# Statistics of two tiles formed at once, one projection moved forward, and new instruction orders in a tuned attention and MLP kernel

## The chip, the cores and the metric

The kernel runs on one core of a Trainium2 chip. The metric is the device time of one execution in microseconds (us). A profile shows one execution; its span leaves out some 2 us that the device time contains.

## The reference

The input has 2048 rows of 448 columns, which the kernel treats as 16 tiles of 128 rows.

```python
def _A_ref(x, wqkv, wo):                    # linear attention, 16 heads of 28
    q, k, v = ...                           # (x @ wqkv), split by head
    phi = lambda t: jnp.where(t > 0, t + 1, jnp.exp(t)) + 1e-6
    pq, pk = phi(q), phi(k)
    kv = jnp.einsum("bhsd,bhse->bhde", pk, v)
    z = jnp.einsum("bhsd->bhd", pk)
    num = jnp.einsum("bhqd,bhde->bhqe", pq, kv)
    den = jnp.einsum("bhqd,bhd->bhq", pq, z)[..., None] + 1e-6
    return (num / den)... @ wo
# [... _B_ref: (gelu(x @ w_gate) * (x @ w_up)) @ w_down, 1792 wide ...]
h = x + _A_ref(_layernorm(x), wqkv, wo)
h2 = h + _B_ref(_layernorm(h), w_gate, w_up, w_down)
```

## The kernel before

The program records every operation as a task of one engine, with the buffers that it reads and writes. `ORDERS` then gives each engine its fixed order of tasks, by number. Waits between engines follow from the buffers. In what follows the tasks are called by their names: `q_t` and `k_t` are the projections of tile t (four matmuls of 448 columns each), `eq_t`, `rq_t` and `ek_t` the functions on ScalarE behind them, `ck_t` and `pk_t` the two steps on VectorE that form phi(K), `pt_t` the product of phi(K) with the normalised tile. `bnst_t` and `bnag_t` are the statistics and their aggregate on VectorE, `ln_t` and `rstd_t` the logarithm and exponential on ScalarE, `negm_t` and `normP_t` the negated mean and the normalisation on GpSimd, `xT_t` the DMA transpose.

```python
def ln_tile(t):
    ln_stats(t, ...)                                   # VectorE: bnst_t, bnag_t
    ln_rstd_act(t, t + 1, ...)                         # ScalarE: ln_t, rstd_t
    if t < N_PE_TR:                                    # tiles 0 to 3
        ...                                            # normalised on VectorE, transposed on TensorE,
                                                       # evicted by ScalarE (evxA_t) and VectorE (evxD_t)
    else:
        ln_negm(t, t + 1, ...)                         # GpSimd: negm_t
        op("pool", ...)                                # GpSimd: normP_t
        G.add("sp", lambda e: e.dma_start_transpose(xnT[:, t, :, :], xnn[:, i, :]), ...)   # xT_t
# [... the projections and phi ...]

# between K and the attention outputs: the denominator and the key-value product
op("act",  ... zbc[B_, :] ...)                         # z1
op("dve",  ... zbc[A_, :] <- zbc[B_, :] ...)           # z0: sum of phi(K), for all partitions
op("dve",  ... pt_sb[A_, 3, :] ...)                    # evpD_3: eviction of the last sums
G.add("pe", fkv, r=b_wv + b_pt, ...)                   # kv: needs all evictions
# [...]
for t in (a, a + 1):
    op("dve", ...)                                     # cq_t, aq_t: phi(Q)
for t in (a, a + 1):
    eng = "dve" if t in T1_DVE else "pool"             # T1_DVE = (0,)
    op(eng, ... t1 = pq[t] * zbc ...)                  # t1d_0 on VectorE, t1p_1 and on on GpSimd
for t in (a, a + 1):
    op("dve", ...)                                     # dr_t: sum by head
    op("act", ...)                                     # deA_t: + eps
    op("dve", ...); op("dve", ...)                     # rd_t, pn_t: pqn = pq / den
# first pair of tiles transposed on TensorE, the others by DMA (oT_p); then out_t = pqnT @ w2
if p == 1:
    dma("sp", wd_sb, B_w_down, ...)                    # dwd: down weights, in program order behind oT_1
# [... second layer norm, hT_t (DMA transpose), gate and up products gu, down products ...]
```

Of the kernel before, what the change touches and what calls it, by code (L numbers as in the profile page):

```python
# [12 lines left out]


ORDERS = (
    "26 32 34 43 63 41 66 71 76 52 59 50 61 79 84 70 87 75 99 83 116 111 91 126 103 138 115 150 162 130 174 142 154"
    " 187 200 213 219 166 229 178 191 245 204 235 217 233 179 249 192 205 218 234 250 254 251 291 257 295 299 293"
    " 260 315 297 266 319 317 263 320 269 278 275 356 333 337 272 434 439 387 444 449 454 459 418 464 506 511 516"
    " 469 526 521 490 472 531 536 578 583 588 562 541 544 593 598 603 608 613 618 623 628 633 638 643 675 648 651"
    " 706 654 657 722 727 732 737 742 747 752 757 762 767 772 777 782 787 804 809 814 819 824 829 795 792 801 798"  # L20
    " 834 839 844 849 854 859 864 869 874 877 880 883 886",
    "3 25 29 30 38 39 33 42 64 47 56 48 57 65 67 72 94 51 95 78 60 106 107 80 77 121 122 86 133 88 85 134 145 146"
    " 100 157 169 158 170 112 118 182 183 195 196 127 139 117 208 209 240 224 241 151 163 225 175 188 201 214 220"
    " 221 230 246 236 237 285 308 288 289 256 253 255 252 312 258 347 351 259 294 316 298 268 318 267 261 265 264"
    " 379 383 262 327 328 270 280 329 330 279 277 271 334 276 273 274 339 435 437 442 414 440 410 445 447 452 450"
    " 457 455 462 460 467 465 482 509 507 486 514 519 512 517 527 529 558 554 524 522 532 534 539 537 579 581 671"
    " 586 584 589 667 591 702 596 594 599 601 606 604 698 611 609 614 616 621 619 626 624 629 631 634 636 641 639"
    " 644 646 723 725 728 730 733 735 740 738 745 743 748 750 755 753 760 758 763 765 770 768 773 775 780 778 785"
    " 783 790 788 807 805 812 810 817 815 822 820 825 827 832 830 837 835 842 840 845 847 852 850 857 855 860 862"
    " 867 865 870 872",  # L30
    "27 28 36 37 31 40 35 44 45 54 46 55 92 49 93 58 104 68 105 73 53 69 62 119 74 120 131 81 132 143 82 144 89 167"
    " 155 90 156 168 101 180 206 102 181 193 113 194 114 222 207 238 128 239 223 129 140 141 340 152 153 164 165 303"
    " 176 341 177 342 304 189 301 190 202 215 302 343 216 203 231 232 372 247 248 373 374 375 286 305 287 307 290"
    " 309 311 310 346 292 350 296 300 352 313 348 314 353 349 321 382 322 378 323 324 405 325 380 331 326 381 332"
    " 335 384 336 385 406 338 357 360 358 403 359 404 361 413 362 438 409 436 443 415 411 441 412 416 475 446 448"
    " 476 367 391 453 451 388 370 392 458 477 547 456 693 463 478 481 461 389 393 390 422 468 466 548 549 485 510"
    " 508 423 487 483 488 484 419 520 518 424 515 550 401 420 513 662 421 398 660 557 528 553 691 429 523 530 555"
    " 663 432 525 694 661 559 470 560 494 491 533 535 556 540 538 692 580 582 670 495 587 473 585 666 590 566 701"
    " 668 496 567 592 563 672 669 564 492 673 565 703 493 704 545 568 597 595 600 602 697 607 605 542 612 610 699"
    " 700 615 617 622 620 627 625 630 632 635 637 640 501 676 647 645 679 504 677 576 649 680 573 681 652 678 710"  # L40
    " 711 642 707 655 708 709 658 712 724 726 729 731 720 717 734 736 741 739 689 746 744 686 749 751 756 754 761"
    " 759 764 766 771 769 774 776 781 779 786 784 791 789 808 806 813 811 818 816 823 821 826 828 833 831 796 793"
    " 799 802 838 836 843 841 846 848 853 851 858 856 861 863 866 868 873 871 875 878 881 884 887",
    "15 13 0 14 1 19 20 21 17 18 16 96 22 97 108 109 123 124 24 135 147 136 148 23 159 171 160 172 184 185 197 198"
    " 242 226 210 211 227 243 306 344 345 376 377 408 407 364 363 365 366 479 369 480 551 395 394 396 397 400 552"
    " 426 425 427 428 431 664 665 696 695 498 497 499 500 569 570 571 575 503 572 682 683 684 685 688 714 713 715"
    " 716 719",
    "2 4 5 6 7 8 9 10 11 12 98 110 125 137 149 161 173 186 199 212 228 244 281 282 283 284 354 386 417 368 371 355"
    " 489 402 399 430 433 471 561 674 474 705 546 502 577 505 574 543 656 721 718 650 653 659 690 687 797 794 803"
    " 800 879 876 885 882 888",  # L50
)


# [117 lines left out]
def bass_sequential_preLN__linear_attn_block__glu_gated_geglu__prompt_kernel(  # L171
# [9 lines left out]
    XN_R, PK_R, HN_R, HR = 10, 8, 4, 8  # L181
    PT_SPLIT = 10
    N_PE_TR = 4
    B1_CHUNKS = [2, 2, 4, 4, 4]
    WARM = 40
    T1_DVE = (0,)
    SEQ = "Q0 K0 K1 Q1 K2 Q2 K3 K4 K5 Q3 K6 K7 K8 K9 K10 K11 K12 K13 Q4 K14 Q5 K15 Q6 Q7 Q8 Q9 Q10 Q11 Q12 Q13 Q14 Q15"

    G = _Graph()
    es = ExitStack()  # L190
    with es:
# [5 lines left out]
        x_sb = sb("x_sb", [128, T, D], BF16)  # L197
# [149 lines left out]
        def ln_stats(t, src_ap, b_src, st, mv, b_st, b_mv, tag):  # L347
            op("dve", lambda e: e.bn_stats(st[:, t, :], src_ap), [b_src], [b_st[t]], "bnst%s_%d" % (tag, t))  # L348
            op("dve", lambda e: e.bn_aggr(mv[:, t, :], st[:, t, :]), [b_st[t]], [b_mv[t]], "bnag%s_%d" % (tag, t))  # L349

        def ln_negm(a, b, mv, nm, b_mv, b_nm, tag):
            op("pool", lambda e: e.tensor_scalar(nm[:, a:b], mv[:, a:b, 0], -1.0, None, ALU.mult), b_mv[a:b], b_nm[a:b], "negm%s_%d" % (tag, a))  # L352

        def ln_rstd_act(a, b, mv, lnb, rs, b_mv, b_ln, b_rs, tag):
            act_exp(lambda e: e.activation(lnb[:, a:b], mv[:, a:b, 1], AF.Ln, bias=eps_t[:, 0:1], scale=1.0),
                    b_mv[a:b] + [b_eps], b_ln[a:b], "ln%s_%d" % (tag, a))
            act_exp(lambda e: e.activation(rs[:, a:b], lnb[:, a:b], AF.Exp, scale=-0.5), b_ln[a:b], b_rs[a:b], "rstd%s_%d" % (tag, a))
# [4 lines left out]
               b_ln[a:b] + [b_mhalf, b_powtmp], b_rs[a:b], "pow%s_%d" % (tag, a))  # L362


        def ln_tile(t):
            ln_stats(t, x_sb[:, t, :], b_x[t], st1, mv1, b_st1, b_mv1, "1")
            ln_rstd_act(t, t + 1, mv1, ln1, rs1, b_mv1, b_ln1, b_rs1, "1")
            i = t % XN_R
            if t < N_PE_TR:
                op("dve", lambda e: e.tensor_scalar(xnn[:, i, 0:D], x_sb[:, t, :], mv1[:, t, 0:1], rs1[:, t:t + 1], ALU.subtract, ALU.mult),  # L370
                   [b_x[t], b_mv1[t], b_rs1[t]], [b_xn[i]], "normD_%d" % t)
                for h, (eng, k0, k1) in enumerate((("act", 0, 2), ("dve", 2, 4))):
                    bk = BK_TR[t % 2][h]

                    def ftr(e, k0=k0, k1=k1, bk=bk):
                        ins = None
                        for k in range(k0, k1):
                            ins = e.transpose(psb[:, bk, (k - k0) * 128:(k - k0 + 1) * 128], xnn[:, i, k * 128:(k + 1) * 128], ident[:])
                        return ins
                    G.add("pe", ftr, r=[b_xn[i], b_ones2, b_ident], w=[b_ps[bk]], name="tr%d_%d" % (h, t))  # L380
                    src = psb[:, bk, 0:(k1 - k0) * 128].rearrange("p (k t) -> p k t", t=128)
                    if eng == "act":
                        op("act", lambda e, k0=k0, k1=k1, src=src: e.activation(xnT[:, t, k0:k1, :], src, AF.Identity), [b_ps[bk]], [b_xnT[t][h]], "evxA_%d" % t)  # L383
                    else:
                        op("dve", lambda e, k0=k0, k1=k1, src=src: e.tensor_copy(xnT[:, t, k0:k1, :], src), [b_ps[bk]], [b_xnT[t][h]], "evxD_%d" % t)
            else:
                ln_negm(t, t + 1, mv1, nm1, b_mv1, b_nm1, "1")
                op("pool", lambda e: e.tensor_scalar(xnn[:, i, 0:D], x_sb[:, t, :], nm1[:, t:t + 1], rs1[:, t:t + 1], ALU.add, ALU.mult),
                   [b_x[t], b_nm1[t], b_rs1[t]], [b_xn[i]], "normP_%d" % t)
                G.add("sp", lambda e: e.dma_start_transpose(xnT[:, t, :, :], xnn[:, i, :]), r=[b_xn[i], b_ones2], w=b_xnT[t], name="xT_%d" % t, kind="dma", after=[two])  # L390
# [43 lines left out]
        lns = 0  # L434
        for what in SEQ.split():
            t = int(what[1:])
            while lns <= max(t, N_PE_TR - 1):
                ln_tile(lns)
                lns += 1
            (k_tile if what[0] == "K" else q_tile)(t)  # L440

        xts = [t for t in G.all if t.name.startswith("xT_")]
# [248 lines left out]
```

## Time and profile before

The kernel before takes 194.37 us (median of 5 runs, 193.93 to 194.69); its profiled execution has a span of 192.2 us.

| engine | busy, us | share of the span |
|---|---|---|
| TensorE | 187.5 | 98% |
| VectorE | 131.7 | 69% |
| ScalarE | 78.1 | 41% |
| GpSimd | 50.6 | 26% |

In a timeline a row is: start, duration, engine, line, operation, the tile written and read, the shapes, the number of instructions joined in the row, and in brackets the idle time ahead of it with its releaser. The last matmul of a row overlaps the first of the next, so starts are compared with starts. TensorE takes its blocks in one fixed order, thus a stop is a difference between two starts that is larger than the matmuls between them need.

### The profile page before, as it was taken

What the parts mean: (1) busy time and instruction counts of PE and PEld (TensorE: products, weight loads), DVE (VectorE), ACT (ScalarE), POOL (GpSimd) and SP (SyncE); (2) the same over time, 40 slices, a digit from 0 to 9 for tenths busy, and PEclk for the clock granted to TensorE, in tenths of its full rate; (3) what the DMA queues carried; (4) which work ended last, traced back from release to release, by engine and by line L of the source; (5) the groups of instructions that cost most, each with busy time, mean ns of one, the idle gap of its engine ahead of it and who ended that gap; (6) DMA issues with size and microseconds to landing.
All of it is one profiled execution on the core that took longest, in us unless ns stands there. A gap on an engine that the chain in (4) does not pass through costs nothing.

```text
span 192.2 us, 4152 instructions
## 1 busy us (share of the span) xinstructions
PE 187.5 (98%) x1572; PEld 108.7 (57%) x1572; DVE 131.7 (69%) x355; ACT 78.1 (41%) x226; POOL 50.6 (26%) x92
## 2 busy tenths in 40 slices
PE   7989999999999999999999999999999999999994
PEld 7544554554778777564444655545556655445454
DVE  2899988999999998979957446736544542244412
ACT  3697836599954243044044420024444420044200
POOL 7068520560263287404190000450000000000000
PEclk9999999999999999999999999999999999999999
DMA  6966558998205866520042124305600001010011
GB/s 192 372 186 82 109 104 172 224 217 122 58 0 112 201 206 124 123 54 1 4 78 46 38 49 95 95 1 124 143 0 3 0 3 46 3 48 3 0 48 48
DMA packets 35331, 16.97 MB, mean 88 GB/s; under 512 B 27696, under 2 KB 34032, under 8 KB 35312
## 3 DMA queue, kind: packets, MB, share of 16 engines
q1 hardware_dynamic: 35168, 16.60, 38.4%
q8 instruction: 12, 0.20, 0.4%
q10 hardware_dynamic: 144, 0.11, 0.2%
q14 instruction: 7, 0.06, 0.1%
HBM read 8.26 MB, written 1.84 MB: 53 GB/s over the span
## 4 chain that ended last, share of the span: by engine, by line
PE 84%; DMA 6%; DVE 4%; ACT 3%; POOL 1%; issue 0%; SPq 0%; DVEq 0%; POOLq 0%
PE ps L603 34%; PE ps L575 22%; PE ps L404 10%; PE ps L423 6%; PE ps L523 5%; PE ps L605 5%; DMA wd_sb<-in_B_w_down_dram 4%; DMA x_sb<-in_A_x_dram 2%; DVE hh L625 1%; DVE st L348 1%; ACT eq L431 1%; ACT pq L432 1%; DVE x_sb L529 1%; PE ps L471 0%; ACT e L415 0%
## 5 line engine op out<-in xcount | busy, mean ns | idle before, releaser
L605 PE MATMUL ps<-hnT,wgu_sb 64*128 64x512 bf16 (+1 forms) x490 | 86.6, 334 | 0.0
L603 PE MATMUL ps<-hnT,wgu_sb 64*128 64x512 bf16 (+1 forms) x490 | 86.4, 333 | 0.1
L623 ACT ACTIVATE gl<-ps 128x256 bf16<-128x256 f32 x112 | 37.1, 380 | 83.7 <-PE ps L605 81.8
L625 DVE TENSOR_TENSOR hh<-ps,gl 128x256 bf16<-128x256 f32 x112 | 42.9, 418 | 30.9 <-ACT gl L623 30.7
L603 PEld LDWEIGHTS ps<-hnT,wgu_sb 64*128 64x128 bf16 x490 | 45.3, 94 | 28.0 <-issue 2.6
L605 PEld LDWEIGHTS ps<-hnT,wgu_sb 64*128 64x128 bf16 x490 | 42.7, 94 | 4.8 <-DVE hh L625 2.0
L575 PE MATMUL ps<-wd_sb,hh 128*128 128x448 bf16 (+1 forms) x238 | 43.6, 342 | 0.1
L575 PEld LDWEIGHTS ps<-wd_sb,hh 128*128 128x128 bf16 x238 | 23.0, 98 | 20.1 <-issue 0.8
L404 PE MATMUL ps<-wqk_sb,xnT 128*128 128x448 bf16 x128 | 27.6, 352 | 0.5 <-ACT xnT L383 0.5
L488 POOL TENSOR_TENSOR t<-pq,zbc 128x448 f32<-128x448 bf16 x15 | 16.6, 1117 | 39.0 <-DVE pq L484 22.2
L579 DVE TENSOR_TENSOR x_sb<-ps,x_sb 128x448 bf16<-128x448 f32 (+1 forms) x17 | 10.0, 591 | 18.2 <-PE ps L575 18.2
L348 DVE BATCH_NORM_STATS2 st<-x_sb 128x6 f32<-128x448 bf16 x32 | 19.3, 612 | 3.7 <-DMA x_sb<-in_A_x_dram 3.7
L404 PEld LDWEIGHTS ps<-wqk_sb,xnT 128*128 128x128 bf16 x128 | 12.1, 98 | 11.6 <-ACT xnT L383 0.8
L423 PE MATMUL ps<-pk,xnn 128*128 128x448 bf16 x64 | 14.1, 352 | 0.0
L523 PE MATMUL ps<-w,pqnT 112*128 112x448 bf16 x64 | 13.6, 353 | 0.3 <-DVE mv L349 0.3
L529 DVE TENSOR_TENSOR x_sb<-ps,x_sb 128x448 bf16<-128x448 f32 x16 | 9.7, 613 | 2.7 <-PE ps L523 2.7
L558 POOL TENSOR_SCALAR hn<-x_sb,nm,rs 128x448 bf16<-128x448 bf16 x14 | 10.5, 755 | 0.8 <-POOL rs L361 0.2
L415 ACT ACTIVATE e<-ps 128x448 bf16<-128x448 f32 x16 | 8.5, 540 | 5.3 <-PE ps L404 5.2
L352 POOL TENSOR_SCALAR nm<-mv 128x1 f32<-128x1 f32 (+1 forms) x19 | 4.1, 220 | 25.1 <-DVE mv L349 24.5
L495 DVE TENSOR_TENSOR pqn<-pq,rd 128x448 bf16<-128x448 bf16 x16 | 9.9, 641 | 0.0
L417 DVE SCALAR_TENSOR_TENSOR pk<-ps,e 128x448 bf16<-128x448 f32 x16 | 9.8, 615 | 0.2
L523 PEld LDWEIGHTS ps<-w,pqnT 112*128 112x128 bf16 x64 | 5.6, 97 | 7.2 <-issue 1.3
(65 smaller groups left out, 130.1 us busy)
## 6 DMA issues: line engine op xcount, KB each, us to landing
out_dram<-x_sb SPq DMA_DIRECT2D x15, 112.0 KB, 1.8
wd_sb<-in_B_w_down_dram SPq DMA_DIRECT2D x1, 1568.0 KB, 7.1
x_sb<-in_A_x_dram SPq DMA_DIRECT2D x3, 448.0 KB, 5.7
wgu_sb<-in_B_w_gate_dram SPq DMA_DIRECT2D x1, 896.0 KB, 12.3
wgu_sb<-in_B_w_up_dram SPq DMA_DIRECT2D x1, 896.0 KB, 16.4
wqk_sb<-in_A_wqkv_dram SPq DMA_DIRECT2D x1, 672.0 KB, 5.0
wgu_sb<-in_B_w_gate_dram SPq DMA_DIRECT2D x1, 672.0 KB, 6.1
wgu_sb<-in_B_w_up_dram SPq DMA_DIRECT2D x1, 672.0 KB, 8.6
```

The lines of the kernel that those rows point to most:

```text
L348: op("dve", lambda e: e.bn_stats(st[:, t, :], src_ap), [b_src], [b_st[t]], "bnst%s_%d" % (tag, t))
L404: ins = e.matmul(ps[:, bk, 0:D], xnT[:, t, k, :], wqk_sb[:, k, c0:c0 + D], start=(k == 0), stop=(k == 3))
L423: ins = e.matmul(ps[:, BK_PT[c], 0:D], xnn[:, t % XN_R, c * 128:(c + 1) * 128], pk[:, ip, :], start=(t == 0), stop=(t == T - 1))
L488: op(eng, lambda e, t=t, n=n: e.tensor_tensor(t1[:, n, :], pq[:, t, :], zbc[:, :], ALU.mult), [b_pq[t]] + b_z, [b_t1[n]], "t1%s_%d" % (eng ...
L523: ins = e.matmul(ps[:, BK_OUT[n], 0:D], pqnT[0:GW, i2, n, g, :], w2[:, g, :], start=(g == 0), stop=(g == NG - 1))
L529: op("dve", lambda e, t=t, bo=bo: e.tensor_tensor(x_sb[:, t, :], ps[:, bo, 0:D], x_sb[:, t, :], ALU.add), [b_ps[bo], b_x[t]], [b_x[t]], "h ...
L558: op("pool", lambda e, t=t, sh=sh: e.tensor_scalar(hn[:, sh, 0:D], x_sb[:, t, :], nm2[:, t:t + 1], rs2[:, t:t + 1], ALU.add, ALU.mult), [b ...
L575: ins = e.matmul(psO, hh[:, j, (t % HR) * 128:(t % HR + 1) * 128], wd_sb[:, j, c0:c1], start=(j == 0), stop=(j == NJ - 1))
L603: e.matmul(psG[:, jj * N:(jj + 1) * N], wgu_sb[A_, k, j * 128:(j + 1) * 128], hnT[A_, ka_, c0:c0 + N], start=(k == 0), stop=(k == NK - 1))
L605: ins = e.matmul(psU[:, jj * N:(jj + 1) * N], wgu_sb[B_, k, j * 128:(j + 1) * 128], hnT[B_, kb_, c0:c0 + N], start=(k == 0), stop=(k == NK ...
L623: G.add("act", lambda e, gi=gi, cs_=cs_, psG=psG: e.activation(gl[:, gi, cs_], psG[:, cs_], AF.Gelu_apprx_tanh), r=[b_ps[BK_G[i]]], w=[b_g ...
L625: op("dve", lambda e, dst=dst, srcU=srcU, srcL=srcL: e.tensor_tensor(dst, srcU, srcL, ALU.mult), [b_ps[BK_U[i]], b_glh], [b_ar[j_][t % HR] ...
```

## The change

From tile 4 on, the logarithm, the exponential and the negated mean are formed for two tiles in one instruction. K of tile 3 goes ahead of Q of tile 2. All engines have new orders. The intent, as I read it, is fewer small instructions and less waiting.

```diff
-    SEQ = "Q0 K0 K1 Q1 K2 Q2 K3 K4 K5 Q3 K6 [...]"
+    SEQ = "Q0 K0 K1 Q1 K2 K3 Q2 Q3 K4 K5 K6 [...]"
+    LN_PAIR = 4
[...]
-        def ln_tile(t):
-            ln_stats(t, x_sb[:, t, :], b_x[t], st1, mv1, b_st1, b_mv1, "1")
-            ln_rstd_act(t, t + 1, mv1, ln1, rs1, b_mv1, b_ln1, b_rs1, "1")
+        def ln_rest(t):
+            if t < LN_PAIR:
+                ln_rstd_act(t, t + 1, mv1, ln1, rs1, b_mv1, b_ln1, b_rs1, "1")
+            elif t % 2:
+                ln_rstd_act(t - 1, t + 1, mv1, ln1, rs1, b_mv1, b_ln1, b_rs1, "1")
+                ln_negm(t - 1, t + 1, mv1, nm1, b_mv1, b_nm1, "1")
+
+        def ln_tile(t, part):
+            if part != 1:
+                ln_stats(t, x_sb[:, t, :], b_x[t], st1, mv1, b_st1, b_mv1, "1")
+                ln_rest(t)
+            if part == 0:
+                return
[...]
-                ln_negm(t, t + 1, mv1, nm1, b_mv1, b_nm1, "1")
+                if t < LN_PAIR:
+                    ln_negm(t, t + 1, mv1, nm1, b_mv1, b_nm1, "1")
[... the caller takes the tiles from 4 on two by two; all of ORDERS, a table of numbers, is new ...]
```

Parts of the new orders, in names instead of numbers (cut):

```diff
 ScalarE, start
-evxA_0 evxA_1 eq_0 ln_2 ln_3 rstd_2 rstd_3 rq_0 ek_0 ek_1 ln_4 evxA_2
+evxA_1 evxA_0 ln_2 rstd_2 ln_3 rq_0 rstd_3 ek_0 ek_1 eq_0 evxA_2
 VectorE, K of tiles 1 to 3
-pk_1 bnag_6 bnst_7 ck_2 bnag_7 bnst_8 pk_2 bnag_8 ck_3 bnst_10 bnst_9 pk_3
+bnst_7 pk_1 bnag_6 bnst_8 bnag_7 bnst_9 ck_2 bnst_10 pk_2 bnag_8 bnag_9 bnst_11 ck_3 bnag_10 pk_3
 VectorE, end of the K phase
-aq_4 cq_5 aq_5 z0 t1d_0 evpD_3 dr_0 evpD_2
+cq_5 aq_4 evpD_3 z0 aq_5 t1d_0 dr_0 evpD_2
 ScalarE, end of the K phase
-z1 deA_0 evpA_0 evpA_1
+z1 deA_0 evpA_1 evpA_0
 DMA queue of SyncE
-oT_1 oT_2 oT_3 hT_2 hT_3 dwd oT_4
+oT_1 oT_2 oT_3 hT_3 hT_2 dwd oT_4
 GpSimd, start
-eps ones wqkpad ident
+wqkpad ones ptpad ident
```

## The prediction

> **What bounds the kernel now.** I read the engine table of the page first, then the waits of TensorE, then each engine's timeline over the first 65 us.
>
> ```profile
> PE 187.5 (98%) x1572; PEld 108.7 (57%) x1572; DVE 131.7 (69%) x355; ACT 78.1 (41%) x226; POOL 50.6 (26%) x92
> PE 84%; DMA 6%; DVE 4%; ACT 3%; POOL 1%; issue 0%; SPq 0%; DVEq 0%; POOLq 0%
> ```
>
> TensorE is busy 98% of 192.2 us, and the chain of work is 84% TensorE. The change removes no matmul, so only idle places of TensorE can give time back. Busy is not the same as full rate, so I compared starts in its timeline: four 448-column matmuls (one projection of a tile, or one product of K with the normalised tile) take 0.76 us from start to start when nothing holds them.
>
> ```profile
> 1.07 4.45 PE L342 MATMUL ps<-ones_bf 128*128 128x128 bf16 x40 [1.07 <-POOL ones_bf L315]
> 9.43 0.84 PE L378 MATMUL ps<-ident,xnn 128*128 128x128 bf16 x8
> 10.79 1.69 PE L404 MATMUL ps<-wqk_sb,xnT 128*128 128x448 bf16 x8 [0.52 <-ACT xnT L383]
> 12.31 0.92 PE L423 MATMUL ps<-pk,xnn 128*128 128x448 bf16 x4
> ...
> 17.61 0.92 PE L423 MATMUL ps<-pk,xnn 128*128 128x448 bf16 x4
> 18.54 0.93 PE L404 MATMUL ps<-wqk_sb,xnT 128*128 128x448 bf16 x4
> ...
> 45.08 2.44 PE L404 MATMUL ps<-wqk_sb,xnT 128*128 128x448 bf16 x12
> 47.77 1.67 PE L523 MATMUL ps<-w,pqnT 112*128 112x448 bf16 x8 [0.26 <-DVE mv L349]
> ```
>
> The reader is to see: from 10.79 us (K of tile 2) the starts follow each other at 0.76 us per four. Up to the end of the K phase, near 36.7 us, the one loss is before 18.54: 0.93 - 0.76 = 0.17 us, K of tile 6 waiting for its transposed tile. Before 47.77 twelve matmuls should take 2.28 us and took 2.69: 0.41 us lost. Later, the chain shows one load that TensorE runs into:
>
> ```profile
> 62.84 0.23 SPq L561
> 63.13 7.13 DMA wd_sb<-in_B_w_down_dram
> 70.30 2.82 PE ps L575 x14
> ```
>
> The down weights start only after the transpose of tile 3 has been issued; the starts around 65.4 and 70.3 us show about 0.35 us lost to the two together. So there is some 0.9 us to win after 10.79, and besides it only the start itself, 0 to 10.79 us, where 16 projections (3.0 us) are done.
>
> **What the Trainium skill says.** "TensorE: Matmul & The Clock Gate", section on the HAM clock gate: the array runs at half rate until a free-running window of about 3.4 us has been busy. The trace agrees: the 40 warm-up matmuls took 4.45 us, 111 ns each, while 14 transposes of the same width later took 0.95 us. Its "Step-by-step" section says that matmuls stay in program order; the order in the diff is thus the order on the array. "ScalarE: Activation LUTs", "What ACT_TABLE_LOAD costs": an activation with a [128,1] bias has a fixed cost of about 280 ns, 186 without it, plus 0.83 ns per element, and neighbours overlap by about 93 ns. The trace agrees with the fixed part:
>
> ```profile
> L355 ACT ACTIVATE ln<-mv,eps_t 128x1 f32<-128x1 f32 x14 | 3.8, 292 | 0.9 <-DVE mv L349 0.8
> L357 ACT ACTIVATE rs<-ln 128x1 f32<-128x1 f32 x14 | 2.7, 200 | 0.2
> L352 POOL TENSOR_SCALAR nm<-mv 128x1 f32<-128x1 f32 x12 | 2.5, 217 | 6.1 <-DVE mv L349 5.9
> ```
>
> A second column therefore costs next to nothing.
>
> **The change part by part.**
>
> *Pairing.* Twelve tiles (4 to 15) become six pairs. Removed: 6 logarithms x 292 + 6 exponentials x 200 = 2.95 us of ScalarE and 6 x 217 = 1.3 us of GpSimd. On ScalarE this matters only between 10 and 16 us, where it is nearly full (4.83 of 5 us from 10 to 15); later it waits for TensorE (5.2 us before the exponentials of K). The price: the first tile of a pair waits for the statistics of the second, one more 0.61 us statistics instruction and its aggregate on VectorE, which is full from 10 to 25 us.
>
> *Where that lands.* Normalised tiles pass to the queue of the DMA transposes, which issues one in 1.26 us:
>
> ```profile
> L390 SPq DMA_TRANSPOSE xnT<-xnn x12: 1253/1264/1900, 11.7 to 27.1; - x12
> ```
>
> Tile 4 left at 11.67. In the new order its normalisation can begin near 11.95, so its transpose leaves near 12.7 and lands 2.5 us later (the usual landing) at 15.2. K of tile 4 is now the seventh block counted from K of tile 2 instead of the sixth, so it needs it near 11.35 + 6 x 0.76 = 15.9 (the start at 11.35 is worked out below). The same sum for tiles 5 to 15 leaves slack everywhere; at tile 6, about 1 us. Gain: the 0.17 us at 18.54, and nothing more, because nothing else waits there.
>
> *K of tile 3 ahead of Q of tile 2.* This only gives TensorE filler while the K products and transposes come. Moving blocks changes no sum.
>
> *The new start.* Two parts cost. First, GpSimd now clears the projection weights' padding ahead of the ones that the warm-up matmuls read:
>
> ```profile
> 0.81 0.20 POOL L315 MEMSET ones_bf<- 128x128 bf16 x1
> 0.95 0.85 POOL L302 MEMSET wqk_sb<- 128x896 bf16 x1
> ```
>
> The warm-up begins near 1.9 instead of 1.07 us and ends near 6.2. All eight transposes of tiles 0 and 1 follow it, partly at half rate, ahead of any projection; K of tile 1 starts near 7.15, and the 16 projections end near 10.2, not 9.43. Second, ScalarE:
>
> ```profile
> 7.64 0.54 ACT L431 ACTIVATE eq<-ps 128x448 bf16<-128x448 f32 x1
> 8.26 0.48 ACT L355 ACTIVATE ln<-mv,eps_t 128x1 f32<-128x1 f32 x2
> 8.65 0.33 ACT L357 ACTIVATE rs<-ln 128x1 f32<-128x1 f32 x2
> 8.88 0.53 ACT L432 ACTIVATE pq<-ps 128x448 bf16<-128x448 f32 x1
> 9.31 0.97 ACT L415 ACTIVATE e<-ps 128x448 bf16<-128x448 f32 x2
> ```
>
> Before, the exponential of Q of tile 0 ran in a hole at 7.64; now it stands behind the two exponentials of K, ahead of the eviction that K of tile 2 waits for. K of tile 0 ends near 9.6, its exponential starts near 9.65, then 0.43 us per instruction: 10.1, 10.5, and the eviction at 10.9 instead of 10.34. One logarithm (0.2 us) has gone from ahead of it, which that figure contains. From eviction start to matmul was 0.45 us, so K of tile 2 starts near 11.35: 0.55 us later, all of it on the path, since TensorE follows without slack. A less lucky phase of the clock window would add to it: I add 0.15.
>
> *Later orders.* The transposed tile 3 and the down weights come some 0.8 us earlier (a residual addition of 0.61 us and a shorter addition that stood ahead of the second of their copies on VectorE now stand behind it), which frees most of the 0.35 us. The down products of tile 3 move between two groups of gate and up products; each change between half-row and full-row matmuls costs about 0.1 us at each side in the starts (1.62 for eight 448-column matmuls against 1.51), so one more break costs 0.2. One reduction now precedes the second pair's normalised queries, 0.53 us later for that transpose; its wait at 47.77 stays about the same, since its landing of 4.1 us was unusually slow: +0.1.
>
> Sum: +0.55 + 0.15 - 0.17 - 0.35 + 0.2 + 0.1 = +0.48, so 194.37 + 0.48, rounded to 194.9 us.
>
> **The rivals.** (a) The pairing frees ScalarE and the K phase speeds up. For: ScalarE is nearly full from 10 to 15 us. Against: TensorE lost 0.17 us there. At most the 0.9 us found above, and with a start as before: 193.3 us. (b) VectorE becomes the bound: waiting for two statistics in a row delays the K products. For: it is 5.00 busy of 5 from 10 to 20 us, and by my sums the product of K of tile 3 comes with no slack. Each late product stops TensorE directly: 0.5 to 1.5 us more, up to 196.5. (c) The later warm-up leaves the first projections at half rate: four cost 1.5 us instead of 0.76, so 0.8 us each time, 195.7 or more. (d) Slow landings. Some transposes took 4.2 us against 2.5; where one hits a tile without slack it costs up to 1 us, in either kernel.
>
> **Range and chances.** The idle that can be won is 0.9 us, 0.5%; faster by 2% needs 3.9 us, which would have to come from a start that the new order makes no shorter. Slower by 2% needs rivals b and c together. The three runs of before differ by 0.76 us. I take 193.4 to 196.4 us; faster 0.02, within 2% 0.95, slower 0.03.
>
> **What would show it.** Six logarithms fewer and a ScalarE busy time lower by some 2 to 3 us with no shorter span; the warm-up starting near 1.9; K of tile 2 near 11.35 instead of 10.79; no idle before K of tile 6; the down weights landing before 70 us; nine groups of gate and up products instead of eight. It would be wrong if K of tile 2 started before 10.8, or if stops of over 0.3 us appeared between 12 and 36 us.

## More of the kernel before

Besides the lines shown in the prediction, two turn out to matter. They are from the timelines of VectorE and of GpSimd, kernel before, near 35 us: each engine multiplies phi(Q) of one tile by the sum of phi(K).

```profile
35.07 0.63 DVE L488 TENSOR_TENSOR t<-pq,zbc 128x448 f32<-128x448 bf16 x1
```

```profile
35.12 1.48 POOL L488 TENSOR_TENSOR t<-pq,zbc 128x448 f32<-128x448 bf16 x1 [9.66 <-DVE zbc L450]
```

The reader is to see that VectorE started first, by 0.05 us, and took 0.63 us. GpSimd took 1.48.

## The result, and the profile after

The changed kernel takes 196.38 us (median of 5 runs, 196.12 to 197.15) against 194.37. The ratio is 1.0116, 95% interval 1.0086 to 1.0146. A ratio here is the mean time of one kernel's fast runs over that of the other's of the same rounds, so it is not quite the ratio of the medians quoted. The loss is 2.0 us, where 0.5 was predicted. The profiled execution of the changed kernel was the slowest of the five, 197.15 us with a span of 195.4. A second profile of the same kernel (run *again*, below) has a span of 193.7. Both are needed, since a stop that stands in one only does not come in every execution.

The engine table and the chain of work on the page of the changed kernel:

```profile
PE 188.1 (96%) x1572; PEld 110.2 (56%) x1572; DVE 132.7 (68%) x355; ACT 75.6 (39%) x214; POOL 50.5 (26%) x86
PE 77%; DMA 6%; DVE 6%; ACT 1%; issue 1%; ACTq 0%; SPq 0%; DVEq 0%
```

ScalarE has 12 instructions fewer and 2.5 us less work, GpSimd 6 fewer, as they should be. TensorE has the same 1572 matmuls. Its share of the chain fell from 84 to 77%, so TensorE waits more. The groups of the window from 10 to 30 us show the pairs: two columns, at 292 ns, which is what one column took.

```profile
L354 ACT ACTIVATE ln<-mv,eps_t 128x2 f32<-128x2 f32 x6 | 1.7, 292 | 0.2 <-DVE mv L348 0.2
```

TensorE's timeline shows where it waits:

```profile
1.83 4.45 PE L341 MATMUL ps<-ones_bf 128*128 128x128 bf16 x40 [1.83 <-POOL ones_bf L314]
...
7.29 3.46 PE L414 MATMUL ps<-wqk_sb,xnT 128*128 128x448 bf16 x16
...
11.77 1.69 PE L414 MATMUL ps<-wqk_sb,xnT 128*128 128x448 bf16 x8 [0.58 <-ACT xnT L392]
...
19.89 0.35 PE L414 MATMUL ps<-wqk_sb,xnT 128*128 128x448 bf16 x1 [0.38 <-DMA xnT<-xnn]
...
40.35 1.00 PE L478 MATMUL ps<-pt_sb,wv_sb 128*112 128x112 bf16 x16 [0.62 <-DVE den L507]
...
57.24 1.67 PE L539 MATMUL ps<-w,pqnT 112*128 112x448 bf16 x8 [0.96 <-DVE rd L510]
```

The reader is to see five places. The warm-up begins at 1.83. K of tile 2 starts at 11.77, not 10.79. K of tile 6 (19.89) waits for its transpose. The key-value product at 40.35 waits where the kernel before did not wait at all. The output product of the second pair of tiles, at 57.24, waits 0.96 us. Here and below the second pair is the second one that DMA transposes, tiles 4 and 5. The releaser named in the last row is not one that the product depends on: by the program it needs two additions on VectorE, done by 54.33, and the DMA transpose of the second pair, oT_2, which was issued at 52.3 and took 4.8 us to land.

To see how the loss grows, here are the starts of seven blocks that have the same work ahead of them in each kernel (from the timelines; *early_mended* is the last experiment):

| block on TensorE, start in us | before | after | again | early_mended |
|---|---|---|---|---|
| K of tile 2 | 10.79 | 11.77 | 11.22 | 10.45 |
| K of tile 6 | 18.54 | 19.89 | 19.27 | 18.60 |
| Q of tile 4 | 28.39 | 29.72 | 29.10 | 28.50 |
| key-value product | 38.23 | 40.35 | 39.73 | 38.34 |
| gate and up of tile 2 | 50.95 | 53.05 | 52.43 | 50.99 |
| output of the second pair | 54.11 | 57.24 | 55.60 | 54.15 |
| first down product | 70.30 | 73.25 | 71.59 | 70.04 |
| span | 192.2 | 195.4 | 193.7 | 191.9 |

Against before, the profile after loses 0.98 us at the start, 0.37 more by K of tile 6, 0.79 more between Q of tile 4 and the key-value product, and 1.03 more ahead of the second pair's output product. *Again* loses 0.43, 0.30, 0.79 and nothing.

**The stop at the key-value product.** VectorE and GpSimd, changed kernel, in two timelines:

```profile
36.48 0.39 DVE L500 TENSOR_TENSOR pq<-pq,eq 128x448 bf16<-128x448 bf16 x1
36.78 1.46 DVE L504 TENSOR_TENSOR t<-pq,zbc 128x448 f32<-128x448 bf16 x1
```

```profile
36.53 1.24 POOL L504 TENSOR_TENSOR t<-pq,zbc 128x448 f32<-128x448 bf16 x1 [10.90 <-DVE zbc L466]
```

The same VectorE instruction that took 0.63 us takes 1.46. In the new order one more addition (`aq_5`, the row at 36.48) stands between the copy `z0`, which releases both engines, and VectorE's product. So GpSimd starts 0.25 us ahead of VectorE and ends at 37.77. VectorE's product ends at 38.24, which is 0.47 after GpSimd's. Behind it come the sum by head, ScalarE's `deA_0` and only then ScalarE's evictions, which the key-value product needs. The Trainium skill, "SBUF — State Buffer", section "Who interferes with whom", says that a VectorE instruction with two SBUF inputs contends with a GpSimd instruction that reads SBUF, and that issue order decides who blocks; it calls the shared pair of ports "an exclusive lock". Both traces agree: 0.63 us on VectorE and 1.48 on GpSimd where VectorE was first, 1.46 and 1.24 where GpSimd was.

**The slow transposes.** Over 17 traces I sorted all 561 DMA transposes by the time from issue to landing. The usual times are 2.5 us for x, 3.05 for the queries and 2.9 for the second layer norm. Seventy took 3.6 us or more, and 69 of these had a packet of the queue "q8 instruction" in flight with them (counted from 1 us after the issue to the landing). Of the 442 without such a packet one was that slow; of the 119 with one, 69 were. The view of the DMA queues of the changed kernel from 15.5 to 17 us shows such a packet (packets, MB, share of 16 engines; then transposes, count and median time to landing):

```profile
q1 hardware_dynamic: 544, 0.13, 43.2%
q8 instruction: 1, 0.02, 5.1%
...
xnT<-xnn SPq DMA_TRANSPOSE x2, 3.2
```

One of the two transposes is tile 6's, 3.93 us from issue to landing. The Trainium skill, "Runtime: NRT & Kernel Launch", section "Instruction fetch mechanics", says that each engine's sequencer refills its instruction memory by its own DMA queue in blocks of 16 KiB, at a cost "mostly hidden". The queue here moved 12 packets with 0.20 MB in either kernel, thus some 16.7 KB each, so I read it as TensorE's refill. What it costs is not hidden when it slows a transpose that has little slack. A packet in flight does not slow every transpose, as *again* shows below.

### The profile page after: what moved, and what is told of

Its sections match the earlier page's. It is cut to its first block, busy times and chain, and to the rows that moved or that the text cites. A ratio compares the mean times of both kernels' runs of the same rounds, so it can differ in the third digit from the quotient of the medians.

```text
span 195.4 us, 4130 instructions
## 1 busy us (share of the span) xinstructions
PE 188.1 (96%) x1572; PEld 110.2 (56%) x1572; DVE 132.7 (68%) x355; ACT 75.6 (39%) x214; POOL 50.5 (26%) x86
## 3 DMA queue, kind: packets, MB, share of 16 engines
HBM read 8.26 MB, written 1.84 MB: 52 GB/s over the span
## 4 chain that ended last, share of the span: by engine, by line
PE 77%; DMA 6%; DVE 6%; ACT 1%; issue 1%; ACTq 0%; SPq 0%; DVEq 0%
PE ps L619 32%; PE ps L591 22%; PE ps L414 7%; PE ps L621 6%; PE ps L539 6%; DMA wd_sb<-in_B_w_down_dram 4%; PE ps L433 3%; DMA xnT<-xnn 2%; DVE den L507 1%; DVE x_sb L545 1%; DVE t L504 1%; DVE st L347 1%; PE ps L478 1%; PE ps L487 0%; DVE hh L641 0%
## 5 line engine op out<-in xcount | busy, mean ns | idle before, releaser
L504 POOL TENSOR_TENSOR t<-pq,zbc 128x448 f32<-128x448 bf16 x15 | 16.7, 1121 | 35.9 <-DVE pq L500 15.6
L574 POOL TENSOR_SCALAR hn<-x_sb,nm,rs 128x448 bf16<-128x448 bf16 x14 | 11.3, 818 | 0.6 <-POOL rs L360 0.2
L511 DVE TENSOR_TENSOR pqn<-pq,rd 128x448 bf16<-128x448 bf16 x16 | 10.8, 687 | 0.0
L351 POOL TENSOR_SCALAR nm<-mv 128x2 f32<-128x2 f32 x13 | 2.9, 226 | 27.5 <-DVE mv L348 27.2
```

The lines of the kernel that those rows point to most:

```text
L504: op(eng, lambda e, t=t, n=n: e.tensor_tensor(t1[:, n, :], pq[:, t, :], zbc[:, :], ALU.mult), [b_pq[t]] + b_z, [b_t1[n]], "t1%s_%d" % (eng ...
L574: op("pool", lambda e, t=t, sh=sh: e.tensor_scalar(hn[:, sh, 0:D], x_sb[:, t, :], nm2[:, t:t + 1], rs2[:, t:t + 1], ALU.add, ALU.mult), [b ...
```

## The experiments

**Theory, after reading the two traces:** the pairing is free. The loss comes from orders: the later start, the lock at the key-value product, and later orders that leave the second pair's transpose without slack. **Rival 1:** the pairing itself makes VectorE or the transposes late, and the stops are its consequence. **Rival 2:** the loss is one cause, the start, and everything behind is only shifted. In the expectations the key-value product has several names; in *mended2* it is called the product of the last K.

### again: the changed kernel once more

No edit.

> The changed kernel, rebuilt without an edit, to see its states again. Its five runs fell at 197.1 (two) and 196.1 to 196.4 (three); the profiled one was a 197.15. Theory: the 0.9 us between them is one wait, TensorE ahead of the second pair's output product (1.03 us in the profiled run), which comes and goes with a slow transpose. If this run falls at 196.2, its profile shows that wait under 0.3 us and still shows the 0.8 us gap ahead of the product of K with V (kv), the late K of tile 2 (11.7 us) and the stop ahead of K of tile 6. Rival: the two states differ at the start, by the phase of the clock; then K of tile 2 would start 0.9 us apart in the two.

Measured: 195.94 us (195.2 to 196.96), ratio 1.0083 (1.0036 to 1.013). The stop of 0.79 us ahead of the key-value product is there again, the one ahead of the second pair's output product is not. The lines of the tile that the query transposes write (last line of its view, time to landing) and TensorE's row, first of the profile after, then of *again*:

```profile
DMA to landing us min/median/max: 3.0/3.1/4.8
```

```profile
DMA to landing us min/median/max: 3.0/3.1/3.4
```

```profile
55.60 1.69 PE L539 MATMUL ps<-w,pqnT 112*128 112x448 bf16 x8
```

With no landing over 3.4 us the same block starts without idle. So this stop comes and goes between executions of one kernel; the lock does not. But it is no rarity: of the 13 profiles of kernels with the change's later orders nine have it, at 1.0 to 1.2 us, and *again*, *early_before*, *half_warm* and *mended* have not. Nor is a fetch in flight enough to cause it. *Again* had one too, begun 2.5 us after this transpose was issued, against 2.8 in the profile after. In 14 of the 17 traces a packet met this transpose. The nine packets that began 2.66 to 2.86 us after the issue go with landings of 4.68 to 4.88 us, the five that began after 2.49 to 2.52 us or after 2.90 with landings of 3.04 to 3.17. Why so little decides, no run shows.

### evict_first: ScalarE's evictions ahead of the step that waits for the lock

```diff
-ScalarE: z1 deA_0 evpA_1 evpA_0
+ScalarE: z1 evpA_1 evpA_0 deA_0
```

> ScalarE's small addition to the first denominator (den) goes behind the two evictions of the K-transpose-x sums instead of ahead of them. Theory (the gap ahead of kv is these evictions held behind that addition, which waits for VectorE's first reduction): the gap of 0.78 us closes to under 0.1, and the time falls by 0.6 to 0.8 us against the changed kernel in the same call. Rival (VectorE's late evictions or the products themselves hold kv): gap and time stay.

Measured: 196.34 us, ratio 1.0107 (1.0067 to 1.0147), no gain. The stop ahead of the key-value product is gone, but one of 0.79 us stands a block later, ahead of the first product with the output weights: that waits for the masked result, on VectorE, which is still behind the long product. Taking away a wait behind the cause moves the stop; the cause is on VectorE.

### old_start: the orders of before up to K of tile 2

```diff
 all engines up to K of tile 2: order of the kernel before, among it
-ScalarE: ... rq_0 rstd_3 ek_0 ek_1 eq_0 evxA_2
+ScalarE: ... evxA_0 evxA_1 eq_0 ln_2 ln_3 rstd_2 rstd_3 rq_0 ek_0 ek_1 evxA_2
```

> The changed kernel with the orders of before on all engines up to K of tile 2 (ones cleared first on GpSimd, transposes between the projections, exponential of Q of tile 0 early on ScalarE); all later orders and the pairing stay. Theory (the start costs 0.98 us): K of tile 2 at 10.7 to 10.9 us instead of 11.77, and the time 0.7 to 1.1 us lower than the changed kernel, if nothing later takes it back; the stop ahead of K of tile 6 may grow, since its transpose cannot start 1 us earlier. Rival (pairing costs, the start only shifts it): K of tile 2 early, but the stops up to the end of the K phase grow by as much and the time stays within 0.3 us.

Measured: 197.16 us (196.61 to 198.22), ratio 1.0149 (1.0108 to 1.019): no faster than the changed kernel. K of tile 2 did start at 10.67, but Q of tile 4 at 29.14, where *again* and *unpaired* have it at 29.10 and 29.22. The gain of 0.5 us was taken back by new stops, 0.41 us ahead of K of tile 4 and 0.54 ahead of K of tile 7. TensorE, and VectorE ahead of it:

```profile
15.70 0.93 PE L414 MATMUL ps<-wqk_sb,xnT 128*128 128x448 bf16 x4 [0.25 <-DVE pk L427]
```

```profile
14.50 0.62 DVE L347 BATCH_NORM_STATS2 st<-x_sb 128x6 f32<-128x448 bf16 x1
15.03 0.60 DVE L427 SCALAR_TENSOR_TENSOR pk<-ps,e 128x448 bf16<-128x448 f32 x1
```

K of tile 4 writes the PSUM bank that VectorE's `pk_2` reads, and `pk_2` (15.03) stands behind two more statistics in the new order than the start can bear. This is the prediction's rival (b), which shows only once the start is early. The stop ahead of K of tile 7 is another matter: that tile was normalised by 15.97, but its transpose was issued at 17.52, 2.2 us behind tile 6's where 1.3 is usual, with a fetch at 15.8. Two more stops stand later in this profile, 1.23 us ahead of the second pair's output product and 0.94 ahead of the first down product. So this run does not tell what the start alone is worth in time.

### unpaired: the changed orders with single statistics

```diff
-    LN_PAIR = 4
+    LN_PAIR = 16
 ScalarE and GpSimd: each ln, rstd and negm of a pair once more, for the second tile, behind the first
```

> The changed kernel with the pairing undone: a logarithm, an exponential and a negation for each tile again, placed next to where the pairs stood, one tile of each pair earlier. ScalarE and GpSimd get back 3.0 and 1.3 us of work. Theory (pairing is off the path of TensorE): the time stays within 0.4 us of the changed kernel. Rival 1 (waiting for two tiles costs the 2 us): at least 1 us faster, with transposes of tiles 4 and 6 leaving earlier and no stop ahead of K of tile 6. Rival 2 (pairing is worth what it saves on ScalarE): 1 us or more slower.

Measured: 196.35 us, ratio 1.0099 (1.0065 to 1.0133), the same as the changed kernel. Rival 1 falls as far as the pairing is concerned: taking it away brings nothing.

### product_early: VectorE's product ahead of the last eviction

```diff
-VectorE: evpD_3 z0 aq_5 t1d_0
+VectorE: aq_5 z0 t1d_0 evpD_3
```

> The changed kernel with one stretch of VectorE's order put back: the copy of the sums (zbc), then at once the first product with them (t), then the eviction of the padded block; in the changed order a residual-free addition stands between copy and product, GpSimd starts its own product 0.26 us ahead, and VectorE's product takes 1.46 us instead of 0.63. Theory (the 0.79 us gap ahead of kv, or ahead of the products after it when the evictions go first, is this slow product and all that queues behind it on VectorE): the product takes under 0.7 us, the gap ahead of kv falls under 0.15 us, no new one appears ahead of the products with wo, and the gate and up products start some 0.7 us earlier relative to kv's predecessor. Rival (the padded block's eviction, or the evictions of ScalarE as such, hold kv): a gap of at least 0.5 us stays.

Measured: 195.02 us (194.2 to 195.45), ratio 1.0060 (1.0025 to 1.0095). VectorE, GpSimd and TensorE of this kernel:

```profile
35.55 0.63 DVE L504 TENSOR_TENSOR t<-pq,zbc 128x448 f32<-128x448 bf16 x1
```

```profile
35.60 1.48 POOL L504 TENSOR_TENSOR t<-pq,zbc 128x448 f32<-128x448 bf16 x1 [10.77 <-DVE zbc L466]
```

```profile
38.70 0.99 PE L478 MATMUL ps<-pt_sb,wv_sb 128*112 128x112 bf16 x16
```

VectorE is first by 0.05 us, its product takes 0.63 us again, and the key-value product starts without idle. The lock is thereby shown as the cause of the 0.79 us. The intervals of the ratios overlap with the changed kernel's, so the size is taken from the profile.

### half_warm: 20 warm-up matmuls of 256 columns instead of 40 of 128

```diff
-    WARM = 40
-    ... matmul(ps[:, 3, 0:128], ones_bf[:], ones_bf[:], ...)
+    WARM = 20
+    ... matmul(ps[:, 3, 0:256], ones_bf[:], ones_bf[:] twice side by side, ...)
```

This leaves nearly the same warm-up time and takes 20 matmuls and their 20 weight loads from TensorE's instruction stream, so a fetch that belongs to a place in that stream comes later.

> The changed kernel with 20 warm-up matmuls of 256 columns in place of 40 of 128: the same time of warm-up, but TensorE has 40 instructions fewer ahead of the work. Theory (a DMA transpose in flight takes 4 us instead of 2.5 when a 16 KB packet of the instruction queue is fetched, and that fetch comes at a fixed count of TensorE's instructions): the slow transpose moves from tile 6 to tile 8 or 9, the stop of about 0.5 us ahead of K of tile 6 goes away (one of up to 1 us may appear ahead of K of tile 8), and the stop of 1.1 us ahead of the second pair's output product goes, since that fetch then comes about 1.1 us later, after its transpose has landed. Rival (transposes are slow by chance or by other DMA traffic): slow ones stay at tile 6 and at the second pair, or move without order.

Measured: 195.76 us, ratio 1.0106 (1.0075 to 1.0137). The first fetch moved from 16.9 us in the profile after to 21.5. Its DMA queues from 15 to 16.5 us, against the lines of the profile after above:

```profile
q1 hardware_dynamic: 544, 0.13, 42.7%
...
xnT<-xnn SPq DMA_TRANSPOSE x2, 2.5
```

```profile
18.07 2.43 PE L414 MATMUL ps<-wqk_sb,xnT 128*128 128x448 bf16 x12
```

The same 544 packets, no instruction packet, a median of 2.5 us, and TensorE takes K of tile 6 without a stop. Tile 6 landed in 2.49 us and tile 10, now with the fetch, in 4.20, where there was slack. So the slow landing follows the fetch, not the tile. The stop ahead of the second pair's output product was absent as well, and no packet met that pair's transpose. The time did not follow: the ratio is that of the changed kernel (1.0116 and 1.0083). The lock was still there (0.79); what else holds the unprofiled runs, up to 195.92, stays open.

### early_before and late_before: one half of the orders each

```diff
 early_before: the kernel before up to the last product of K, then the later orders of the change
 late_before:  the changed kernel up to the last product of K, then the later orders of before
```

> The kernel before, unpaired, with its own orders up to the last K product and the changed orders behind it. Theory (the 2 us are about half early, half late): K of tile 2 at 10.8, Q of tile 4 at 28.4 as before; then the gap ahead of kv of 0.8 us, and the stop ahead of the second pair's output product of up to 1.1 us where it falls on the fetch; time 0.8 to 1.7 us over before. Rival (all comes from the start and the K phase): within 0.3 us of before.

> The reverse: the changed kernel, paired, with its own orders up to the last K product and the orders of before behind it. Theory: Q of tile 4 at 29.1 to 29.7 as in the changed kernel, no gap ahead of kv, and the end 0.7 to 1.2 us over before. Rival (all comes from the later orders): within 0.3 us of before.

Measured: *early_before* 194.74 us, ratio 1.0053 (1.0027 to 1.008); *late_before* 195.53 us, ratio 1.0087 (1.0049 to 1.0125). Each half costs by itself, so rival 2 falls. But neither half has the lock. In *late_before* VectorE's order at the key-value product is before's. In *early_before* the cut left `aq_5` ahead of the copy `z0`, VectorE's product took 0.62 us, and the gap of 0.8 us that was expected did not come. So the two losses, 0.5 and 0.9%, are not parts that must add up to the 1.16 or 0.83% of the whole change. In *late_before* K of tile 6 stops by 0.74 us. In *early_before* the down weights are the loss: the first down product stops by 1.15 us.

### mended and before_half_warm: two remedies together, and one in the kernel before

```diff
 mended:           product_early and half_warm together
 before_half_warm: the kernel before with 20 warm-up matmuls of 256 columns
```

> The changed kernel with the two edits that closed a stop each: VectorE's product straight behind the copy of the sums, and 20 warm-up matmuls of 256 columns. Theory: both gains stand beside each other, so no gap ahead of kv, no stop ahead of K of tile 6 nor ahead of the second pair's output product; what is left of the loss is the start (K of tile 2 at 11.2 to 11.8), less where later waits were: 0 to 0.6 us over before. Rival (a closed stop opens the next one): still 1 us or more over before.

> The kernel before with 20 warm-up matmuls of 256 columns and nothing else. Theory (instruction fetch makes transposes slow): the slow transpose leaves tile 6 for tile 8 to 10, so the stop of 0.18 us ahead of K of tile 6 goes; the first output transpose lands in 3.1 us instead of 4.1, and the stop of 0.42 us ahead of the second pair's output product goes; time 0.3 to 0.8 us below before. Rival (the fetch only moves the stops to other places): within 0.2 us of before.

Measured: *mended* 195.95 us (194.91 to 196.79), ratio 1.0122 (1.0079 to 1.0166), which is a miss. *Before_half_warm* 194.97 us, ratio 1.0051 (1.0014 to 1.0088), a miss too. In the second the reason is visible: the first fetch moved, but the one at 44.2 us stayed, the transpose of the queries with it took 4.64 us, and TensorE stopped 0.97 us ahead of the output product of tiles 2 and 3 (which this expectation and the prediction call the second pair's), against 0.42 in the kernel before. Shifting a fetch frees one transpose and may hit another. In *mended* the lock's stop is gone (key-value product at 39.09), but K of tile 2 started at 11.48. Why its unprofiled runs reach 196.79 stays open, since a run without a profile shows no place; the kernel before spread more than usual in these rounds too, from 193.0 to 195.05.

### ones_first and evict_ahead: the two parts of the start, one look each

```diff
 ones_first:  GpSimd: eps ones wqkpad ident ... as before
 evict_ahead:
-ScalarE: rstd_3 ek_0 ek_1 eq_0 evxA_2
+ScalarE: rstd_3 ek_0 ek_1 evxA_2 eq_0
```

> The changed kernel with only GpSimd's first memsets in the order of before, so that the warm-up can start at 1.1 instead of 1.8 us. Theory (late warm-up, then 16 projections in a row): K of tile 2 0.3 to 0.5 us earlier than the 11.2 to 11.8 of the changed kernel, 10.8 to 11.3. Rival (ScalarE's order alone sets K of tile 2): no change.

> The changed kernel with the eviction of the transposed tile 2 ahead of the exponential of Q of tile 0 on ScalarE, nothing else. Theory: the eviction starts 0.43 us earlier unless its transpose is not done; the transposes end near 10.5 to 11 us, so K of tile 2 comes 0.2 to 0.4 us earlier relative to the end of the projections: the gap between the transposes and K of tile 2 falls from 0.75 to about 0.4 us. Rival: VectorE's half of the eviction holds it, and the gap stays.

Measured, a single run each: 196.0 and 197.36 us. In *ones_first* the warm-up began at 1.07 again, and K of tile 2 still started at 11.40: the transposes wait for the normalised tile 1 at 5.9 us, so the later warm-up cost nothing there. In *evict_ahead* the eviction came at 10.82, and K of tile 2 at 11.70. It needs the PSUM bank of Q of tile 0, which `eq_0` reads, and that now ran from 11.10 to 11.65. So the late exponential itself delays K of tile 2; which of the two stands first made no difference in this one look. In the kernel before it ran at 7.64, in a hole.

### mended2: three early places put back

```diff
 the orders of before up to K of tile 2 on all engines, and
-VectorE: bnst_7 pk_1 bnag_6 bnst_8 bnag_7 bnst_9 ck_2 bnst_10 pk_2 bnag_8 bnag_9 bnst_11 ck_3 bnag_10 pk_3
+VectorE: pk_1 bnag_6 bnst_7 bnag_7 ck_2 bnst_8 pk_2 bnag_8 bnst_9 bnag_9 ck_3 bnst_10 pk_3 bnag_10 bnst_11
-VectorE: evpD_3 z0 aq_5 t1d_0
+VectorE: aq_5 z0 t1d_0 evpD_3
```

> The changed kernel with three places of its early orders put back: the orders of the kernel before up to K of tile 2 on all engines; on VectorE the products and copies of K of tiles 1 to 3 each behind one statistics at most, not two; and VectorE's product in the mask ahead of the last eviction, as in the run product_early. The pairing, K of tile 3 ahead of Q of tile 2 and all later orders stay. Theory (the early loss is the start, the order of statistics on VectorE and the lock between VectorE and GpSimd, and these add up once all three are put back together): K of tile 2 at 10.7 us, no stop ahead of K of tile 4 (it was 0.41 with the old start alone), none ahead of the product of the last K (0.79 in the changed kernel), Q of tile 4 at 28.4 to 28.8 against 29.14 with the old start alone; what is left is the stop ahead of the second pair's output product, 0 to 1.1 us as it falls. Median 194.2 to 195.2, 0 to 0.5% above the kernel before. Rival (they do not add up, because the transposes or a fetch of instructions then set the pace of the K phase): Q of tile 4 still at 29.0 or later with a new stop between 12 and 28 us, median 195.5 or more.

Measured: 195.3 us (194.34 to 196.05), ratio 1.008 (1.0043 to 1.0118), just above the expected median. In the profile the early part did add up: Q of tile 4 at 28.43, key-value product at 38.27, gate and up of tile 2 at 50.96 against 50.95 before. One expectation failed: K of tile 4 stopped by 0.59 us. In this execution the first fetch fell at 12.7 us and tile 4's transpose took 3.67. Behind 51 us the loss is the later orders': 1.03 us ahead of the second pair's output product and 0.88 ahead of the first down product.

### early_mended and mended2_again: with and without the later orders of before

```diff
 early_mended:   the early orders of mended2 up to the end of the K phase, then the later orders of before;
                 pairing, K of tile 3 ahead of Q of tile 2 and the new order of the K phase on TensorE stay
 mended2_again:  mended2, in the same rounds
```

> The changed kernel with the old orders up to K of tile 2, VectorE's K products of tiles 1 to 3 each behind one statistics at most, and the later orders (from the mask on) of the kernel before; left of the change are the pairing, K of tile 3 ahead of Q of tile 2 and the order of the K phase on TensorE. Theory (what was lost lies in those three sets of orders, nothing in the pairing or in the moved K): K of tile 2 at 10.3 to 10.8 us, Q of tile 4 at 28.3 to 28.8, no stop ahead of the product of the last K, no 1.0 us stop ahead of the second pair's output product (at most the 0.2 to 0.5 of the kernel before), down weights landing before 70.8; ratio to the kernel before 1.000, between 0.996 and 1.004. Rival (pairing or the moved K costs by itself, or the costs do not add up): ratio 1.006 or more, as with the early places alone put back (1.008).

> The same kernel as mended2, in the same rounds as early_mended: its difference from early_mended is the later orders alone. Expected 1.008 (1.004 to 1.012) of the kernel before, K of tile 2 at 10.3 to 10.8, gate and up of tile 2 at 50.8 to 51.3, and the stops of 1.0 ahead of the second pair's output product and 0.9 ahead of the first down product again (or absent, in which case its time is nearer 1.004).

Measured: *early_mended* 194.03 us (193.67 to 194.51), ratio 1.0036 (1.0017 to 1.0054); *mended2_again* 195.07 us (194.37 to 195.84), ratio 1.0084 (1.006 to 1.0108). The intervals do not overlap, so the later orders cost 1.04 us by the medians of the same rounds, 195.07 - 194.03. TensorE of *early_mended*, then of *mended2_again*:

```profile
10.45 1.75 PE L414 MATMUL ps<-wqk_sb,xnT 128*128 128x448 bf16 x8 [0.36 <-ACT xnT L392]
...
54.15 1.69 PE L539 MATMUL ps<-w,pqnT 112*128 112x448 bf16 x8
```

```profile
19.93 0.93 PE L414 MATMUL ps<-wqk_sb,xnT 128*128 128x448 bf16 x4 [0.99 <-DMA xnT<-xnn]
```

The first has the start and the second pair's output product of the kernel before (54.11). The second is the same program as *mended2*, whose first fetch fell at 12.7 us. Here it fell at 17.8, tile 4 landed in 2.51 us and tile 7 in 4.07, and TensorE stopped at K of tile 7 instead (the row at 19.93). So where a fetch falls is not the program's alone; it differs between executions.

The ratios that belong together, each to the kernel before of its own rounds:

| early orders | later orders | ratio |
|---|---|---|
| of the change | of the change | 1.0116, 1.0083 |
| of the change | of before | 1.0087 |
| of before | of the change | 1.0053 |
| mended | of the change | 1.008, 1.0084 |
| mended | of before | 1.0036 |

No version tried beats the kernel before. What keeps *early_mended* 0.36% above it stays open: its profiled execution, the fastest of its six, shows stops of the kernel before and one of 0.52 us at K of tile 4, whose transpose took 3.59 us with a fetch at 12.9.

## Why the prediction was right or wrong

The direction and the class (same within 2%) were right, and 196.38 us lies just inside the range. The size was wrong: 2.0 us where the sum gave 0.48. By its steps:

1. **The bound** was right. TensorE in its fixed order sets the end, the change removes nothing from it, and all of the loss is idle time between its blocks.
2. **The pairing** was right. ScalarE's work fell by 2.5 us (2 to 3 predicted) and the span did not; without it the time is the same (*unpaired*).
3. **The start, +0.55 and +0.15,** was nearly right: 0.98 us in the profile after and 0.43 in *again*, 0.70 predicted. The mechanism, the exponential of Q of tile 0 behind those of K, is what happens, though it delays K of tile 2 through its PSUM bank as well as through the eviction (*evict_ahead*). The part laid to the later warm-up was wrong as far as one look shows; *ones_first* gave it back and K of tile 2 still started at 11.40. Undone alone the start brought no gain in time: VectorE's statistics then bind at K of tile 4, and that run had later stops besides (*old_start*). The "16 projections" of the prediction are 16 matmuls, four projections.
4. **The gain of 0.17 us at tile 6** had the wrong sign. The step said "leaves slack everywhere; at tile 6, about 1 us", and took the usual landing of 2.5 us. Tile 6 landed in 3.93 us, and K of tile 6 lost 0.37 us against before (0.30 in *again*). Where the landing was usual, the stop was indeed gone (*half_warm*). The prediction had slow landings as rival (d), but in its sum they cost nothing, since it took them as equal luck for either kernel. They come with the fetches of instructions. The prediction's own sign of being wrong, a stop of over 0.3 us between 12 and 36 us, thus appeared: by the starts K of tile 6 stopped 0.54 us, and 0.43 in *again*.
5. **The end of the K phase** is where the prediction failed outright. It says of the moved projection that "Moving blocks changes no sum", goes on to the start and then to tile 3 and the down weights, and has no term between. An addition moved between a copy and VectorE's product let GpSimd start first, and the lock made that product 1.46 us long: a stop of 0.79 us in every run that has this order, shown by *product_early*. The prediction compared orders on TensorE and on ScalarE, and did not ask which of two engines that start at the same release would be first.
6. **The later orders, -0.35 + 0.2 + 0.1,** had two terms mis-sized and left one stop out. From the second pair's output product to the first down product took 16.01 us in the profile after and 15.99 in *again*, instead of 16.19 before: a gain of 0.2 us where 0.35 was predicted. Behind that some 0.2 us were lost in both, as the term of +0.2 said. The gain was small because the down weights, issued 0.38 and 1.32 us earlier (counted from gate and up of tile 2), took 8.35 and 8.26 us to land instead of 7.13. The chain of the profile after shows the load, and TensorE behind it:

```profile
64.85 8.35 DMA wd_sb<-in_B_w_down_dram
73.25 2.82 PE ps L591 x14
```

In the three profiles the weights landed 4.9 to 5.2 us after the landing of the last transpose ahead of them (65.3 before, 68.0 after, 66.7 in *again*). In the new order this is tile 2's and no longer tile 3's. So it seems to be that transpose, not the issue, that sets them; no run took it apart. The term of +0.1 was for tiles 2 and 3, with the wait at 47.77. Their transpose did leave 0.50 us later, counted from the key-value product, but it landed in 3.05 us (3.44 in *again*) instead of 4.09, and the wait of 0.42 us was gone; smaller waits ahead of it took nearly all of that back. The sum has no term for the next pair, tiles 4 and 5, called the second pair here. Its transpose left at 52.3 for a use at about 56.2, so a usual landing of 3.05 us has 0.8 us of slack. In the kernel before it left at 49.9 for a use at 54.11 and had 1.2. A landing of 4.76 us overran the smaller slack by 1 us, and so it did in nine of 13 profiles. In time the later orders, without the lock, cost 1.04 us in *mended2_again* against *early_mended*, and 0.5% in *early_before*.

In the profile after the pieces make up the span's difference: 0.98 + 0.37 - 0.02 + 0.79 - 0.02 + 1.03 + 0.07 = 3.2 us, block by block as in the table, where 0.07 is all behind the second pair's output product. In *again* they are 0.43 + 0.30 - 0.02 + 0.79 - 0.02 + 0.01 + 0.01 = 1.5 us in the same order. The medians of the changed kernel's two series, 2.0 us and 1.5 above before, lie between those two profiles.

## What to carry to other kernels

Where one instruction releases VectorE and GpSimd together, and both then read SBUF, keep the one that others wait for first in its queue: one short addition in between cost this kernel 0.8 us. A DMA transpose with 1 us of slack or less stopped the array here in many executions, because its landing can grow from 2.5 or 3 to over 4 us when a fetch of instructions falls on it; the longest of the query transposes, 4.88 us against 3.05, would have asked for 1.8 us. When a change is a new order on all engines, look at each place where two engines share something, and not only at the engine that is the bound; and undo the parts together, since one remedy alone can be swallowed by the next limit (*old_start*, *mended*).

## What the Trainium skill lacked or had wrong

- "Runtime: NRT & Kernel Launch", "Instruction fetch mechanics", calls the cost of a refill "mostly hidden". It lacks that DMA transposes are often slow with such a packet in flight: 69 of 119 transposes with such a packet took 3.6 us or more from issue to landing, against 1 of 442 without, and the usual time is 2.5 to 3.05 us. It also lacks that the moment of a refill differs between executions of one program (12.7 and 17.8 us in *mended2* and *mended2_again*).
- "SBUF — State Buffer", "Who interferes with whom", agrees with the traces on the lock. The numbers to add: 0.63 us for a 128x448 product on VectorE that started first, 1.46 for one that started 0.25 us after GpSimd's; GpSimd's took 1.24 where it was first and 1.48 where it was second.
- "DMA: Bandwidth & Descriptors" has a section on the DMA transpose. In the pages I looked at I found no time from issue to landing for a small one: 2.5 us from issue to landing for a tile of 128 by 512 alone. Nor did I find how a load behind a transpose lands: here one of 1568 KB landed 4.7 to 5.9 us after the transpose issued ahead of it had landed (17 traces).
